# A new order table for a fused attention and GLU kernel, drawn up with later bank-free times

## The chip, the cores and the metric

One core of one Trainium2 chip runs the kernel. The metric is the device time of one execution in microseconds (us), as the median of repeated runs; a lower number is better. The profile is one further execution, traced by the hardware profiler.

## What is computed

Two branches read the same x (2048 tokens by 512 features, fp32) and are mixed by a gate:

```python
q = (x @ wq), 32 heads of 16;  k = x @ wk;  v = x @ wv      # one k and v for all heads
a = softmax(q k^T / 4) v, heads side by side, @ wo
b = (sigmoid(x @ w_gate) * (x @ w_up)) @ w_down              # 1792 hidden features
g = sigmoid((x * gate_w).sum(-1))
out = g * a + (1 - g) * b
```

## The kernel before

**Tiles and stages.** The tokens are cut into 4 blocks of 512. The 32 heads are cut into 8 groups of 4, which gives 32 units (block, group). For one unit the keys are cut into 16 chunks of 128. TensorE (PE) does five kinds of work, always into one of the eight PSUM banks of 128 x 512 fp32:

- `project` (L854): keys, values and queries from x, 12 full matmuls of 128 x 128 weights for each bank. It happens in the first 80 us only. The order calls it G.
- `maximum` (L1132): scores of one head, laid so that VectorE (DVE) can take the row maximum with one TENSOR_REDUCE (L1134). 2048 half matmuls, each on 64 rows of the array.
- `scores` (L1141): the scores again, transposed, with the maximum taken off inside the matmul. ScalarE (ACT) writes their exponentials p (L1143). Also 2048 half matmuls.
- `fill` (L1106): the GLU products and the output projection, 4404 half matmuls in chains of 12 to 36 that add up in one bank. ACT reads a finished bank of the gate product (L1115), DVE one of the up product (L1121), and ACT (L1082) or DVE (L1063) one of the products that go to the output.
- `pv` (L1005): p times the values, 4 matmuls of 32 columns for each chunk (the trace has two records for each). The order calls a chunk V. Chunks that follow each other without other work form a run and add up in one bank of their own. At the end of a run ACT copies that bank out (`finish`, L1012), and GpSimd (POOL) adds the copy to the unit's sum (`add_sums`, L1019). The copies of a unit after its first have two buffers (`vp`).

The three kinds of half matmuls use the upper or the lower 64 rows of the array, and two of them run side by side as a pair, one on each half. A chunk of `pv` uses all 128 rows and 32 columns at a time.

**What sets the order.** The string `ORDER` (L668) has one character for each step of PE. V and G are told above. A hexadecimal digit issues a pair: its quotient by 4 is the work of the upper half and its remainder that of the lower, with 1 for `maximum`, 2 for `scores`, 3 for `fill` and 0 for nothing. A point issues nothing. `plan` (L716) walks this string with the class `State`, which books a time in units of its own for each of PE, DVE, ACT, POOL and SyncE (SP). It decides from these bookings which bank is taken (`take`, L190: the one that comes free first, and it must be free by the booking), who empties a bank, and where the work of the other engines and the DMAs fall between the steps. The instructions of each engine then stand in this order, and semaphores guard every bank. So the bookings decide an order and nothing else; no time of the chip comes out of them.

**When a bank counts as free.** In `issue_m` (L512) and `issue_s` (L522) this stands as

```python
self.free[i] = self.on("dve", self.now + LATE, RED) + TAIL + FREE          # maximum, L516
at = self.on("act", self.now + LATE_A, EXP) + TAIL_A; self.free[i] = at + FREE_A   # scores, L528
```

`LATE` and `LATE_A` are the units from the issue of a matmul until DVE or ACT may begin, `RED` and `EXP` what the reader takes, `TAIL` and `TAIL_A` its end, and `FREE` and `FREE_A` a margin on top. `settle` and `gather` (L428, L458) use the same margins for the banks of `fill`, and `release` (L554) uses `FREE` for the bank of a run. The step of a run needs a bank that is free and four p of its chunk (`can_v`, L535).

Of the kernel before, what the change touches and what calls it, by code (L numbers as in the profile page):

```python
# [663 lines left out]


ORDER = (  # L668
    "GGGGGGG555G55G555G55......5G55GG555G55G555GG55G555GG5dddGff7f77ffffd757d.GG7fffdfffd7f7ffffdedee7edef7ef7b7b7b7b"
    "bdfedebdfbdb79ffef55VVVV7b76bfdbf9fbdef9fe7ededee7f6f7bdef6fdff7775VVV9deedef7edf9fbe77bfb7bb7bdff9edb7fedfd75dV"  # L670
    "VVVVGV6fede.edfef7efbb7f9fb7b7b7bfed9fbdb7fedbfed7d5VV655VVV7b7bb7fededbf9e7fbdededeef77b7ef9faf7d7f7ddVVVV5bb77"
    "bbbffde79fefededeede7bf77bfbd6fff7ddd5VVV566VV6ddefe7eedf6fbfe7b7b7b7bbdfbdfededbb7fedbf5VV555VVV97b7fbdbdbfb7eb"
    "fdedededeef76ffb76fef9f6fbf5V5a6V996VV696V559VVV7b7b7bbfdbdbedfe7edeeddee7fb7fed6feedf7777bVVVV9deeedf7fedb7bdef"
    "b7b7bb77eefddeedfef9b7ffdbddfedd5VVVVV6e9ff77bfb7b7bb77bfedbbdf6ff9f9ff.dd66VV659VV659VV7b7b7bbdfedbedfe79feedde"
    "e7f6f7bf9fbf6f6ffd5VVVVV7b97b7bbfdf9fee7efdedeede77efdbe7fee7feedfbdbfed9dVVVVV56fbfe7bfb7b7bb77bfbdafdbdf7bfedf"
    "de.56VV65aV6a5V955VVV97bbb77ffbdbdee7fededeede7f7b7bbfdbf9fbfb7e7aff775VVVV9dedfbdee7fedeeddef6fe7e7e7bfdbff775."
    "5VVVVV9deff9f6fbd6fedefb7b7b7bbdff9f9bf7ef97edefaV65eVVV959VV677bbfdfeeddee7f6ff797VVVdede7efb7b7b7bedbdff9eVVVd"
    "edede7ef6f6fbf97bfb7bb7bdff9f6efdbf6dbeff615.VVVVV6deededf7bf6feb7fbdb7bb7bbdfdfbdb7ef6edf5fdVVVVV5edeef7bfe7ede"
    "7e7bfb7b7bbdff9dbf6f9fedbf6fdV5a6V9aaVVVVV6dedef7ef6f6fbdbfb7e727b7bdef9fdbfbdef9f6f6f.9VV955VVV6edff6defb7ed6fb"
    "fe7b7bb7bdedfedfb7bf97edbfd4.9VV656VV5a5VV97bfdbdbe7f6fedefe7e763b7befdedefdbdefb7b79f.5VVV9a5V595VVV7b7afdedbf7"  # L680
    "b79fefbdedeedee77ff6f9fe7edb7bf7V95aV669V99aVV695VVV7b7afdf97efedef6fedb7b7bbdff96ffbd6fbffddd5VVVV677bbb7fdbfed"
    "bf6fededeede77fbfba7fdbf7fddd5VVVV767bbb7bffdedbe7fedededee7fb7f6ef7edbfd7f79VVVVV97bbb77fdef9f6fedefbde4ee7defe"
    "7dbf9fbb7f9ff55.VVVVVV7b79bffa7fdebdb7fededeedef7f6fe7e7bf9f9f6f7VVV969VV6edeedf7fb79fee7f9fb7b7bb7bfdedfbdef9f6"
    "ffd545.VVVVV96edffb7bf7edb7bbfdedeede7ef7defe7ebdb7bbf9VVVVV5baV9b7b7bb7fdfe7bedfedededee7ff6f67bfbdbfd7fd5VVVVV"
    "5edeeedfb7f6fe7bef7bb7b7bfddeefdbdbfa7f7eebV996V965VV5a9VV6a5VV6dedef7bfb79fbf9fb7edeede7ef7e7efdef97b7ffedefedd"
    "9VVVVV69f7bff6fb7b7bb7b7f9fedebdbf79ffefe5.6VV955VVV9b7b7fdbfb79fee7fededeede7ef7deef7ef67bffd9ffdedd5VVVVV67b7f"
    "bf9b7fe7b7bb7fededeedf7bbbd7ff5.5VVVVVdedede6ff6fb7bdb7efb7bb7bdef7edfedbf97bfed715.VV59aVVVV7b7bb5fee7fbdebdfbd"
    "eededef7b7fb7b79ff5efeedVVV659VV5bbb7fefdedede7efb7bf7b7b7VVV9fdeeddeedfe7b7be7V956VV977bbb7ffbd9fedbfedededee77"
    "fb7bfb7bf9fd7bfe7fbf67aVVVVV97defedefe7edeededfb7ef6f6fdbef7b79.dbVV955VVV7b7bb79b7ff9feedfededeede7fe76ffbdbf6b"
    "dff75V559VVVVV56efbfedf6fbd6fbfbde7b27bdfed7ebf7ededbfbfb.55VVVVV7b79b7fbfed6f9fedbfededee77ef7bdbfbfa7ffdd6Va95"  # L690
    "VV56aVVV5b7b7bfbdefb79fedefededee7f7bf6f9fb7bdefef.645VVV996V59aV569VVV7b7bb5fefbdb7bedfedededee77fbb7fb7bbddeed"
    "f5ca.VV666V59aV655VVVdede7ebdbf76fedbfe7b7b7bbdff9bdbfdb7eedeff585.VVVVV56b7.bfefdef9f6fedefb793bb7b7fbd6ff9eff9"
    "efdee5VV566VVVV5b7bb7fbdef9fb7eefdededeedbf7f6f6fafd7bff79VVVVV977b7bfeefd6fbf9f9fedeede7f7ef6fbd9fbf6ff75VVVVV9"
    "e9dff7ef6f9fef67efb7bb7bddfb9ffbde7ef9bffbfb67777VVVVV5bbfededefdededeed.7efb7edbfb7bdfbdf55VV655VVV67befdf9fb7b"
    "f6f9dbfeedede7ffe7b7bf9f6fbdef5VVVVV5b7bb7fef9f6fef9dbfedeede7fe77b7ef9fbf6ffddedeeedeVVVVV69fb7fb7fe7b7bb7b7f9f"
    "bdbdbef7f9efde.6eVV65aV9a5V596VVVV7b7bb7fededebde7f9fbd6ceedf7eef7bdbb7deb7fdb.5VV659VVV97b7bfdbf9fe7eb7defedede"
    "dbbf77bfe7e7edefbf2.65VV595VVVdedededeef7e7b7bb7fb7b.7bbdfbdb7edeed7feff7515VVV955VVV66fbfdf6fbdb7bdbfe7ededee7f"
    "f97eefdbf6dbbbf6VVVVV5eeffb7efbde7eedbf7b7b7b7eff9f9dbf9ffedf7d5VV569VVVV6b7bb7bfdfdbdbe7efdedeedef76ffe7bbf5bfa"
    "fd7dVVVVV7b7bbfdedededefb76ff75VVdede6ffb7b7b7bf9fefe5dVV79bb7b7bffdaf5fefededeede7fb7fbde76fbf9faf5c5.VVVVV6ded"
    "defbef76fef9fb7b7b7bbdf9ff6f9fbb7dedef5c9.VV666V5a9VVVV977bbbfdfbde7edbfe7eddeee7ff6f9faf7dbfe7bf6VVVVVV977bbfde"  # L700
    "bfdbdb7efbdedeede7bf77ebfdee77efbf15.5VVVVV59effb7bbf79fbf9fededdeee7fb7fb6f7eed7edbfbVV6a6VVVV5bbbfdb7def9faf7b"
    "fdedeeddf6fefe6f76fbef7bbbV969V5a5VVVVV6deeedf7dbf6fbb7fbde7b87bdfeddbfe76fefbdf7b.9aVV65aV95aVVVV6deeedf7ef7bd9"
    "fbfe7b7bb7bdedff97bfede7f7fd5VV556VVVdedeedfe7e7e7bdbfb7b7b7bbfddbefdbdbf6fedf75VV659VVV5aeff7edfedb7b7ef.edb7b7"
    "b7bfe7bfd9bdfbededf5c9VV666V65aV595VVVdedeb7bfde7e7efbfdb7b7bbdfedef6dbf6fef7f575VVVVdedee9dff6f6f9fbfb7b7b7bbdf"
    "edbdeef5fefe75VV97b57VVVVdededeedfe76fbbf7b7bb7b7bdf9ffedbbd7bdffdd5VV56aVV97b7fe7ef9fb79fefe7edeede7ffb6dfef9f6"
    "fbfb75VV555VVVVdede9fe7fb7e7edbbfdb7bb7bdff9b7efd6fef6ffdededddeeVVVVV67bf7e7efb7b7bb77bfbdafdedfedf9ff775.aVV96"
    "aVVVV5edeef7bdefbdee7fb7b7b7bbdbfddbfbd6fedeff75V655VVVVdeded6efe7fb79fefb7b7bb7bdfdef9fb7ef9dbfef616.VVVVV6dede"
    "dfb7ef6fe7bef7b7bb7bdbdfbddbfaf7deffd4a5.VV655VVVV5eededefbf7e7bdbdbfb7bb7bdfedee7dfef67bfbfa15.VV655VVVV59effb7"
    "bdbfede7bfb7edeede7f6fbdfe7eed7ffedbdafedbdVVVVV6f6b7fb7fbdb7b7bb7fbdbbddedefb7ebfde.aV6a6VV996V56aVVVV9ededffb7"
    "b7b7bdeedf6fbVVVdededbfb7b7bb7fbfedee6V56aVVV5b7bbb7fdbfafddbfededeede77effe7bdee7bb7fd5.35VVVVVdededeedef7e7bb7"  # L710
    "fb7b7bb7bdfdbe7dbfbdbf6eefe.2aVVaaaVVVaaaVVVbfbffbefefeebaVVeeeefffffbbbbaVVaaaVVaaaVVeefefbfffebaVVbbbbbfffafff"
    "eeeVaaaVVaaaVVeeffffbb8VVV"
)


# [532 lines left out]
```

## Time and profile before

| | |
|---|---|
| median of 3 runs | 1585.42 us (1584.21 to 1585.45) |
| the profiled execution | 1584.35 us, its span 1582.4 us |
| busy, share of the span | PE 99%, DVE 85%, ACT 77%, POOL 50% |
| instructions | 12910 matmul records, 2280 on DVE, 2415 on ACT, 713 on POOL |
| granted TensorE clock | 1.00 of full speed |

The 1.95 us between the span and the execution's own time lie around the program. A busy PE in this profile is a PE with some matmul under way, so waits inside a stream of matmuls must be read from the start times in the timeline and from the weight loads (PEld), whose idle time before them is recorded with its releaser.

### The profile page before, as it was taken

To read this page: it belongs to the slowest core of one execution; us is meant where nothing else is said; L and a number is where in the kernel's file an instruction comes from. 1 tells how busy PE (TensorE), PEld (TensorE's weight loads), DVE (VectorE), ACT (ScalarE), POOL (GpSimd) and SP (SyncE) were. 2 spreads that over 40 slices of the span, in tenths; PEclk is the share of its full clock that TensorE was granted. 3 is DMA by queue.
4 is the path that set the end of the run, shared out by engine and by line. 5 is a ranking of instruction groups with operands and counts; after the bars stand their busy time and mean duration, and the time that the engine had idled before them with its cause. 6 is when DMAs were issued, how large, how long until landed. Compare 5 with 4: busy or idle time off the path is not lost.

```text
span 1582.4 us, 33531 instructions
## 1 busy us (share of the span) xinstructions
PE 1572.6 (99%) x12910; PEld 1026.3 (65%) x12910; DVE 1337.5 (85%) x2280; ACT 1223.7 (77%) x2415; POOL 786.0 (50%) x713
## 2 busy tenths in 40 slices
...
DMA packets 62839, 102.94 MB, mean 65 GB/s; under 512 B 24412, under 2 KB 24668, under 8 KB 62680
## 3 DMA queue, kind: packets, MB, share of 16 engines
...
q14 instruction: 58, 0.48, 0.1%
...
## 4 chain that ended last, share of the span: by engine, by line
PE 97%; DVE 1%; ACT 0%; DMA 0%; SPq 0%; issue 0%; POOL 0%; DVEq 0%; ACTq 0%
PE bank L1106 33%; PE bank L1005 29%; PE bank L1132 17%; PE bank L1141 15%; PE bank L854 2%; DVE mx L1134 1%; SPq L967 0%; DMA qs<-qd 0%; DVE q L947 0%; ACT x L781 0%; PE bank L1187 0%; DVE x L787 0%; DMA wkv_raw<-wkv 0%; POOL wkv_s L757 0%; DVE wkv_stack L885 0%
## 5 line engine op out<-in xcount | busy, mean ns | idle before, releaser
L1134 DVE TENSOR_REDUCE mx<-bank 128x1 f32<-128x512 f32 x2048 | 1251.1, 681 | 173.1 <-PE bank L1132 109.5
L1143 ACT ACTIVATE p<-bank 128x512 f32<-128x512 f32 x2048 | 1036.7, 653 | 4.6 <-PE bank L1141 1.1
L1141 PE MATMUL bank<-qs,ks 64*128 64x512 f32 x2048 | 721.5, 400 | 0.0
L1132 PE MATMUL bank<-ks,qs 62*128 62x512 f32 x2048 | 682.5, 408 | 0.2 <-DMA qs<-qd 0.2
L1005 PE MATMUL bank<-p,v_aug 128*32 128x512 f32 x4096 | 477.5, 597 | 0.0
L1132 PEld LDWEIGHTS bank<-ks,qs 62*128 62x128 f32 x2048 | 338.3, 184 | 131.8 <-issue 50.9
L1141 PEld LDWEIGHTS bank<-qs,ks 64*128 64x128 f32 x2048 | 360.7, 185 | 83.4 <-ACT p L1143 18.4
L1012 ACT COPY ou<-bank 128x512 f32<-128x512 f32 x194 | 116.8, 602 | 281.9 <-PE bank L1005 195.6
L1019 POOL TENSOR_TENSOR ou<-ou,ou 128x512 f32<-128x512 f32 x163 | 210.0, 1288 | 210.8 <-ACT ou L1012 209.1
L1005 PEld LDWEIGHTS bank<-p,v_aug 128*32 128x32 f32 x4096 | 114.5, 109 | 254.6 <-issue 208.7
L1106 PE MATMUL bank<-wd,hl 64*128 64x512 f32 x1344 | 279.4, 392 | 0.1
L1106 PE MATMUL bank<-x,wu 64*128 64x512 f32 x1344 | 278.7, 391 | 0.0
L1106 PE MATMUL bank<-x,wg 64*128 64x512 f32 x1344 | 275.6, 392 | 0.0
L1106 PEld LDWEIGHTS bank<-wd,hl 64*128 64x128 f32 x1344 | 205.2, 185 | 19.7 <-issue 4.2
L1106 PEld LDWEIGHTS bank<-x,wg 64*128 64x128 f32 x1344 | 203.2, 185 | 16.8 <-issue 2.0
L1106 PEld LDWEIGHTS bank<-x,wu 64*128 64x128 f32 x1344 | 204.8, 185 | 14.3 <-issue 1.7
L1085 POOL TENSOR_TENSOR ba<-ba,pa_d 128x512 f32<-128x512 f32 x31 | 39.6, 1285 | 103.2 <-ACT pa_d L1082 103.2
L830 POOL CAST wg<-rg 128x1024 fp32r<-128x1024 f32 x27 | 28.1, 1039 | 124.8 <-PE bank L1106 69.1
L757 POOL TENSOR_TENSOR wd<-rd,wd 128x512 fp32r<-128x512 f32 x56 | 72.4, 1292 | 4.5
L757 POOL TENSOR_TENSOR hl<-h,hl 128x512 fp32r<-128x512 f32 x56 | 72.0, 1286 | 4.5
L1106 PE MATMUL bank<-wa,o 64*128 64x512 f32 x360 | 71.5, 393 | 0.0
L830 POOL CAST wu<-ru 128x1024 fp32r<-128x1024 f32 x27 | 28.1, 1040 | 82.4 <-PE bank L1106 76.1
...
## 6 DMA issues: line engine op xcount, KB each, us to landing
...
```

The lines of the kernel that those rows point to most:

```text
L757: lo.tensor_tensor(hl[:, 1, :], raw, f32(hl[:, 0, :]), op=ALU.subtract)
L830: nc.gpsimd.tensor_copy(WS[item][:, 0, :], raw)
L854: nc.tensor.matmul(ps, w[:, p, part(kc)], X[b, kc][:, q, :], start=i == 0, stop=i == 3 * KC - 1)
L1005: nc.tensor.matmul(ps[32 * j:32 * j + 32, :], v_aug[:, c, :], PT.pop((u, c, j)), start=start, stop=stop)
L1012: nc.scalar.copy(to, ps)
L1019: nc.gpsimd.tensor_tensor(SUMS[u], SUMS[u], PARTS_OF[u].pop(0), op=ALU.add)
L1085: nc.gpsimd.tensor_tensor(BA[b, t], BA[b, t], PA[b, t].pop(0), op=ALU.add)
L1106: ins = nc.tensor.matmul(banks[i], l, r, start=start, stop=stop)
L1132: nc.tensor.matmul(banks[i], qs_t[u % 3][r, pr, part(qt)], ks[r, kb * 512:(kb + 1) * 512], start=True, stop=True)
L1134: nc.vector.tensor_reduce(MX[u][:, pr, h, qt, kb:kb + 1], banks[i], axis=AX.X, op=ALU.max)
L1141: nc.tensor.matmul(banks[i], ks[r, part(c)], qs_t[u % 3][r, pr, :], start=True, stop=True)
L1143: nc.scalar.activation(p, banks[i], AF.Exp, scale=0.25)
```

## The change

Five of the planner's numbers are raised (`LATE` by 2 units, `LATE_A` by 4, `FREE` by 35, `FREE_A` by 5, `RED` by 2), and the string `ORDER` is another one, for which each `take` holds under the new numbers. The reference, the tiles, the functions that issue instructions and the number of matmuls stay. The diff, cut:

```diff
-LATE, LATE_A, FREE, FREE_A = 188, 196, 30, 55
+LATE, LATE_A, FREE, FREE_A = 190, 200, 65, 60
...
-RED, GATED, SUM, ENDS, INVERSE, LOWER = 258, 258, 285, 115, 70, 285
+RED, GATED, SUM, ENDS, INVERSE, LOWER = 260, 258, 285, 115, 70, 285
...
 ORDER = (
-    "GGGGGGG555G55G555G55......5G55GG555G55G555GG55G555GG5dddGff7f77ffffd757d.GG7fffdfffd7f7ffffdedee7edef7ef7b7b7b7b"
...
+    "GGGGGGG555G55G555G55........5G55GG555GGG555G55G555GG55Gff5fdfffff7ff75d..ddffffffff75fd7GG755Gb7bfedbbd7bfe7bdfe"
...
```

In the characters of the string: 512 V and 24 G stand in both. The runs of V are 182 before and 197 now; stretches of V or G, each with digits on both sides, are 193 and 209. Steps with one half alone (a digit with 0 on one side) are 26 and 4, points 43 and 15. The rows of each engine are as many on PE and SP, four fewer on DVE, 19 more on ACT and 19 more on POOL. All line numbers behind the string are lower by one in the changed kernel.

**Place one: PE, unit 20 (block 2, group 4), `pv` of chunks 8 to 12.** In a row of `pv`, p_9_0_1 is the tile of chunk 9 and head pair 0, 1. Before, one run holds chunks 8 to 12; the stretch from chunk 9 to chunk 10 reads

```order
L1005 MATMUL bank_79<-p_9_0_0_13631,v_aug 32x512
L1005 MATMUL bank_79<-p_9_0_1_13619,v_aug 32x512
L1005 MATMUL bank_79<-p_9_1_0_13624,v_aug 32x512
L1005 MATMUL bank_79<-p_9_1_1_13594,v_aug 32x512
L1005 MATMUL bank_79<-p_10_0_0_13647,v_aug 32x512
L1005 MATMUL bank_79<-p_10_0_1_13665,v_aug 32x512
L1005 MATMUL bank_79<-p_10_1_0_13640,v_aug 32x512
L1005 MATMUL bank_79<-p_10_1_1_13654,v_aug 32x512
```

and now

```order
L1004 MATMUL bank_76<-p_9_1_0_13621,v_aug 32x512
L1004 MATMUL bank_76<-p_9_1_1_13673,v_aug 32x512
L1131 MATMUL bank_79<-ks,qs_108 128x512
L1131 MATMUL bank_77<-ks,qs_108 128x512
L1131 MATMUL bank_72<-ks,qs_108 128x512
L1140 MATMUL bank_73<-qs_109,ks 128x512
L1140 MATMUL bank_74<-qs_109,ks 128x512
L1131 MATMUL bank_75<-ks,qs_108 128x512
L1004 MATMUL bank_78<-p_10_0_0_13685,v_aug 32x512
L1004 MATMUL bank_78<-p_10_0_1_13709,v_aug 32x512
L1004 MATMUL bank_78<-p_10_1_0_13641,v_aug 32x512
L1004 MATMUL bank_78<-p_10_1_1_13702,v_aug 32x512
```

The run ends behind chunk 9, three pairs of half matmuls follow, and chunk 10 begins a new run in another bank. Each end of a run brings one more copy on ACT (L1012 before, L1011 now) and one more addition on POOL.

**Place two: PE, the same unit, the run that holds chunks 2 to 4 before and 1 to 5 now.** Before, the last rows ahead of the run and its first row are

```order
L1106 MATMUL bank_77<-x_1_9220,wg_5_12653 128x512
L1106 MATMUL bank_78<-x_1_9220,wg_5_12653 128x512
L1106 MATMUL bank_77<-x_1_9220,wg_5_12653 128x512
L1132 MATMUL bank_76<-ks,qs_108 128x512
L1106 MATMUL bank_77<-x_1_9220,wg_5_12653 128x512
L1132 MATMUL bank_73<-ks,qs_108 128x512
L1132 MATMUL bank_72<-ks,qs_108 128x512
L1132 MATMUL bank_75<-ks,qs_108 128x512
L1132 MATMUL bank_74<-ks,qs_108 128x512
L1132 MATMUL bank_79<-ks,qs_108 128x512
L1005 MATMUL bank_78<-p_2_0_0_13292,v_aug 32x512
```

and now

```order
L1105 MATMUL bank_72<-x_1_9247,wg_5_12715 128x512
L1140 MATMUL bank_76<-qs_109,ks 128x512
L1131 MATMUL bank_74<-ks,qs_107 128x512
L1105 MATMUL bank_78<-x_1_9247,wg_5_12715 128x512
L1105 MATMUL bank_72<-x_1_9247,wg_5_12715 128x512
L1105 MATMUL bank_78<-x_1_9247,wg_5_12715 128x512
L1131 MATMUL bank_77<-ks,qs_108 128x512
L1105 MATMUL bank_78<-x_1_9247,wg_5_12715 128x512
L1140 MATMUL bank_73<-qs_109,ks 128x512
L1131 MATMUL bank_79<-ks,qs_107 128x512
L1004 MATMUL bank_75<-p_1_0_0_13328,v_aug 32x512
```

Before, the run takes bank_78, whose last writers are the gate products (L1106) a few rows above it, so that ACT must have read the gate out of it (L1115). Now the run begins one chunk earlier and takes bank_75, which no row shown above it writes; the gate's banks here are bank_72 and bank_78.

## Rows read from the trace of the kernel before

**Rows 1.** The page of before: span and busy time of each engine.

```profile
span 1582.4 us, 33531 instructions
...
PE 1572.6 (99%) x12910; PEld 1026.3 (65%) x12910; DVE 1337.5 (85%) x2280; ACT 1223.7 (77%) x2415; POOL 786.0 (50%) x713
```

**Rows 2.** The page of before: shares of the chain that ended last, by engine.

```profile
PE 97%; DVE 1%; ACT 0%; DMA 0%; SPq 0%; issue 0%; POOL 0%; DVEq 0%; ACTq 0%
```

**Rows 3.** Windows: us, busy of PE, PEld, DVE, ACT, POOL (x instructions), then clock.

```profile
600.00:1000.00 400.00, 399.95 (x3361) 262.82 (x3360) 348.05 (x591) 318.70 (x633) 199.50 (x180) 1.00 0.19 61
```

**Rows 4.** Timeline, PE, 705 to 711.7 us: start, us, instruction, merged count.

```profile
705.02 1.92 PE L1005 MATMUL bank<-p,v_aug 128*32 128x512 f32 x16
706.88 0.50 PE L1132 MATMUL bank<-ks,qs 62*128 62x512 f32 x2
707.21 0.40 PE L1141 MATMUL bank<-qs,ks 64*128 64x512 f32 x1
...
707.45 0.40 PE L1141 MATMUL bank<-qs,ks 64*128 64x512 f32 x2
707.78 3.64 PE L1005 MATMUL bank<-p,v_aug 128*32 128x512 f32 x32
711.35 0.50 PE L1132 MATMUL bank<-ks,qs 62*128 62x512 f32 x1
...
711.69 0.39 PE L1141 MATMUL bank<-qs,ks 64*128 64x512 f32 x1
```

**Rows 5.** Waits of PEld, ACT: us in total, times, longest.

```profile
PEld bank L1005 <- ACT p L1143: 22.6, 72, 0.9
PEld bank L1132 <- ACT p L1143: 22.1, 46, 0.8
PEld bank L1132 <- DVE mx L1134: 22.1, 38, 0.8
PEld bank L1141 <- ACT p L1143: 18.4, 36, 0.8
...
ACT ou L1012 <- POOL ou L1019: 15.2, 13, 2.4
...
PEld bank L1141 <- DVE mx L1134: 11.7, 35, 0.8
PEld bank L1005 <- DVE mx L1134: 10.6, 31, 0.4
```

**Rows 6.** Timeline, PEld, 1423.6 to 1425.5 us, around a run of two chunks.

```profile
1423.63 0.16 PEld L1005 LDWEIGHTS bank<-p,v_aug 128*32 128x32 f32 x8 [0.24 <-ACT gs L1115]
...
1425.48 0.18 PEld L1132 LDWEIGHTS bank<-ks,qs 62*128 62x128 f32 x1 [0.84 <-DVE mx L1134]
```

**Rows 7.** Timeline, 1050.4 to 1051.4 us, a run that waits for its bank.

```profile
1050.46 0.94 PE L1132 MATMUL bank<-ks,qs 62*128 62x512 f32 x5
1050.55 1.15 ACT L1115 ACTIVATE gs<-bank 128x512 f32<-128x512 f32 x2
...
1051.33 0.16 PEld L1005 LDWEIGHTS bank<-p,v_aug 128*32 128x32 f32 x8 [0.36 <-ACT gs L1115]
```

**Rows 8.** Timeline, 947.5 to 948.2 us, a pair that waits for its bank.

```profile
947.57 0.39 PE L1106 MATMUL bank<-x,wg 64*128 64x512 f32 x1
...
947.85 0.18 PEld L1132 LDWEIGHTS bank<-ks,qs 62*128 62x128 f32 x1 [0.21 <-DVE mx L1134]
...
948.19 0.39 PE L1141 MATMUL bank<-qs,ks 64*128 64x512 f32 x1
```

**Rows 9.** Timeline, PEld, the first and the last wait of that kind.

```profile
114.97 0.18 PEld L1141 LDWEIGHTS bank<-qs,ks 64*128 64x128 f32 x1 [0.16 <-DVE mx L1134]
...
1244.28 0.18 PEld L1132 LDWEIGHTS bank<-ks,qs 62*128 62x128 f32 x1 [0.19 <-DVE mx L1134]
```

**Rows 10.** Groups by line and form: busy, mean ns | idle before, releasers.

```profile
L1012 ACT COPY ou<-bank 128x512 f32<-128x512 f32 x194 | 116.8, 602 | 281.9 <-PE bank L1005 195.6 <-issue 32.7 <-POOL ou L1019 15.2
L1019 POOL TENSOR_TENSOR ou<-ou,ou 128x512 f32<-128x512 f32 x163 | 210.0, 1288 | 210.8 <-ACT ou L1012 209.1
```

More of the change, by code (lines that the diff above doesn't have):

```diff
@@ L668 @@
 ORDER = (
-    "GGGGGGG555G55G555G55......5G55GG555G55G555GG55G555GG5dddGff7f77ffffd757d.GG7fffdfffd7f7ffffdedee7edef7ef7b7b7b7b"
[L670 to L712, printed above, removed]
+    "GGGGGGG555G55G555G55........5G55GG555GGG555G55G555GG55Gff5fdfffff7ff75d..ddffffffff75fd7GG755Gb7bfedbbd7bfe7bdfe"
@@ new lines @@
+    "dedeedfe76fee7fedbfbb777.5VVVV9dedef7bf9f6fee7f9fb7bb7bdfbdfbd6fef7ffdd55VVV656VV6ddefb7efbde7eedfb7b7bb7bdf9fbd"
+    "f6feeedffb79VV555VVV97bfe7edf9fe7bb7fbdededee7f6ffe7edbf7ff7755VVVV6fdedef9f9fedeb7fb7bb77bbfd9ffbdb7ef9fddf5dVV"
+    "VVV67fb7bbdfb7ef6bdefdedeedef7e7fb7bf6f9fffd55VVVV7b7b7b7bfed9fbdedefedeede7f7b7efe7bedf5f5f7VVVVVdededb7efe7eed"
+    "7bfb7b7b7bbfd9fbdf6fef97fdfd5VV695VV566VVdedeedef7b7e7bf9f9f7bbb7bffde7edbfed6fbff55VVVV6a5V9edef7def6f6fedb7bfb"
+    "7b7bbdf9ffbdbde7ef6fed7V599VV566VVV9edef7f9fe7ef6edb7fb7bb7bfdbdbdfede7bfe7f5dVV695VV596VVdedb7bfe7bbd7bf9ffeded"
@@ new lines @@
+    "ee77bfb7bdee7fed6ff57VVVVVdedededefb7ee77bbf7b7b7bbfd9fbfd9fb7effede5VV655VVV977b7bfef9f9fb7efededeede7f6ff6fbdb"
+    "edff7b79V5a9VV566VVV5ededefbfb79fef6f6f7bbb7bfddef9fb7bdbfdddf6VVVVV7b7bb5fbfed6fbf9fededeedef7b77bfe7eedfb76fdV"
+    "659VVVV696Vdede5eeffe7bb7defb7b7bb7bdfdbfedeb7dbfedb7dVVV655VVV97b7fbfededeed7bf6fafbVVVdedeef7b7b7bb7fededf57VV"
+    "dede6edff6fb7edbbf7b7b7bbdff9fbdedefa7fdf57VVVVV7b7b7bbdf9fbde7efededeede7f6ffb7edefdf7bb57VV955VVV96dffe7efbd6f"
+    "eb7fedb7b7bbfdbdeef7dbfb7edfe5V9a6VVVV56aV6ddefbdefb76fede7bf7bbb7bfddebdfef9e7effb75VV596VVVVdedee6dffb7ef6f9fb"
@@ new lines @@
+    "7b7b7bbfdf9dbfbdeee7fff95Va5aVV695VVV5b7b7bfefbdeb7ed7efedeede7fed7efb7bf9fefbb9V569VV656VV599VV97b7fe7bfbdaf7f9"
+    "efdededee7f6f7bfe7bdefe7f97V965VV96aVV996VVV9ef7f97bfbbd7bfedfededee7e7f6fbf6dbfbdb7f5dVV655VVV5b7bfedbf9f6fbf6f"
+    "9fededee7fe7dbfb7edfff7795VVVV977bbff9fedaf7f97efedeedef76ffe7bdbf97bffd5VVVV7b79fedbfe7edb7bfbdededee7fb7bf7b7b"
+    "deffde5dVVVVV7b7e7ef9f9fb7bed7efededee7fb7fbdb7b7efdd5feVVVV65aVV5edefbe7f6f9fe7bfedb7b7bbdf9ffb7bdefbdfded6V696"
+    "VV6a9VV6a5VVVdedeedef76f6fbf6fb7b7bb7bdfedfedbedbdfb76f7VVVV9deedff6fede7be7fb7b7b7bbfdbdfed9fbdefff755VVV956VVV"
@@ new lines @@
+    "7b7bb5fbfbd9fedef6fedeeddefb7fb7e7ee7dbfbf5VV965VVV5eef7edefe79fbf6fbdbb7bb7fdfbdbdb7efedffd55VVVV767bfbdbfedbf6"
+    "f6fbdedeede7f7efb79fbbde7fef9VV656VVVV5edefedefb7ee7f9fb7b7b7bbdfdedbfe7bf97ffdd6VV695VVVV97b7fedbfb79fbedf6fede"
+    "dee7f6ffe7edefbfb7b79VV595VVb779bffbdebdfe76ffededee7fb79feb7dbfede7f75VV9a6VVVVdededee7f6fbf6dbfb7b7b7bbfd9fbdf"
+    "bde7bfede7dVVV656VV596VVdedef6fb7b7b7bdbfedef9VVV7b7bfbdededeedfb7bff65VV976ffbdefb7bf9f9e7fededeef7e7edfb7bb7fb"
+    "d9feV955VVVV5b7bfb7bfedb7eedfe7edededef6f7bfe7bfa7ffd75VV95aVVVVde9def7bfb7b7bf9fe7edeedef7e7efde7bfb97ff75VV955"
@@ new lines @@
+    "VVV7bdef6f9fbde7edefe7b7b7bbdfedfed6fb7bbffee9V965VVVVV6ddeedeff6fb7ef6bf7b7bb7bdfbdfededefb9f7f79V966VVVV59aV7b"
+    "7b7bfbd9fafde7fedeeddee7f7bfedee7b7f9f6f7VV959VV5a6VVVdadbf7edfe7af7defe7b7b7bb7fbdefdededbef7f5bV999V654aVV5aaV"
+    "V659VV7b7b7bbfd9fede7bfedededeef7f6fe7edeff7b7779VVVV5ededefbfedbbde7fb7b7bb7bfdf9bfdb7ef5ffddd5VVV656VV5edeeef7"
+    "fbdef6bdb7fb7bb7bdf9ffbdb7eedb7fdedVVVVV767bfee7f9fedbb7fe7eddeedfbf6fb7bf9dedff77aV565VVVVVdede6ffb79fe7edbf6fb"
+    "b77bbdff9f9f9fe7bfefee9V659VVVV977bb7fbfedebdb7fededeede7fe7ef7b7eddfd77b7VVVVV97fbf9f6f9fb7bdbfededeedef7b7b7fb"
@@ new lines @@
+    "db7efefed5VV655VVVde6edf7efbdbf6f97efb7bb7bfddefb7edbf97effd6V969VVVVV7b7bdbfed6fbf6bdfbdeeddee7fb7fb79fbf6fefee"
+    "5VV5a9VVVV7b5bfb7bfedb7edbfedededeef7e7ef7bdef7fd7775VVV599VVdede6f7efbde7ebdfb7b7b7bbfd9fedf6fbedeffb7aV955VVVV"
+    "797bfe7ef9f9fb7efbdedededef6fef7b7b7efe7f79VVVVV9dfb7ebdfb7bdb7befdeddeee7fb7f6f6fef9fbfbd9VV665VV569VVVdedaf7f6"
+    "fedaf7bdfe7b7bb7bdfedfb7bdbf6ffded9V666VVVVVdedededefb76feb7fb7b7b7bbdf9ffbdb7efbdede7dVVV655VVeddeef7b7b7b7bfbd"
+    "eefe5VVVdedeef7b7bb7b7f9ffded5VV97bb7b7ff9feedf97efedeede7fb77bfede7edf7d77VVVV6ddedefefb79fedbfb7b7bb7bfdbdb7fe"
@@ new lines @@
+    "def9fe7f5eVVV695VVde5eedfefe76fbf6bf7b7bb7bfddbefd9fbdefe7f79V659VV56aVVVV9edef7f6f9fef6defb7b7bb7bfdbdbfdbdef6f"
+    "bdef5VV656VVVVdededef6f6feb7f9fb7b7b7bb7fbdfed9fbdbdeffe5V996VVVV7b677bfbfbdedeb7fededeeddbf7bfb7e7ef6fedbebV69a"
+    "VV966VVVVV5edeeefdfb7edb7efb7b7b7bbfd9ffedbdb7efbdf5eV6a6VV59aVV695VV96ffbdb7fbdb7bf6fedeedeedbf77fbf6fbdede7f75"
+    ".VV955VVV7b7bb77bfbdedfdefededede7efe7bde7bfe7ff7759VV959VV5b7bbb7ff9fedeb7fededeedef76ffe7edbfbdb7f57VV955VVV69"
+    "9V9b7fe7defb7bf9f6f9feedede7f6ff6f9fee7fb76f7VVVV999VVdedeeddee7fbf97bbf7b7bb7bf7fe6dfeedf9fefbb5VV569VVV6edef7d"
```

7 lines of the change are left out of this document (added).

## The prediction

> **What bounds the kernel now.** I read the page first, then the chain, the windows, the waits, and last the timeline around single events. The page shows PE busy for 1572.6 of 1582.4 us, far ahead of DVE (1337.5) and ACT (1223.7) [rows 1], and 97% of the chain that ended last is PE's own [rows 2]. In the middle of the kernel PE is busy for 399.95 of 400 us at a granted clock of 1.00, which is the 2.4 GHz level [rows 3]. So the time is the length of PE's own stream. Three things make it up: the matmuls themselves, the changes between pairs (two halves of the array) and chunks of `pv` (column strips), and the weight loads that stand before a bank which DVE or ACT has not emptied yet. The change leaves the first alone, adds to the second and can take from the third. How the other engines share their time matters only where PE waits for them.
>
> **The matmuls.** Their number is the same: 8500 half matmuls, 512 chunks, 24 steps of projection. What falls is the number of steps with one half alone, from 26 to 4. If every lone half cost a whole step, 22 of them would be 11 pairs less, at 0.24 us each from start to start (707.21 to 707.45) [rows 4], or 2.6 us. At the other end is nothing, since each half of the array has its own stream and the partner of a lone half can begin the next step early. I take 0.2 us off, near that end, because the count of half matmuls is what fills PE. The points (43 to 15) issue nothing and cost nothing by themselves.
>
> **The changes between pairs and chunks.** There are 193 stretches of chunks or projections between pairs before and 209 now, 16 more. A run of two chunks takes 1.86 us to the next pair (705.02 to 706.88) and one of four 3.57 us (707.78 to 711.35), so a chunk is 0.855 us [rows 4]. From the start of the last pair ahead of the run of four to the second pair behind it are 4.24 us (707.45 to 711.69); two pairs at 0.24 and four chunks at 0.855 would be 3.90. A run therefore costs **0.34 us** for its two changes [rows 4], and 16 more cost 16 x 0.34 = **+5.4 us**, wholly on the path. The Trainium skill speaks against the change here: by "TensorEngine Tiling (Array Packing)", section "Key Properties", a change of tiling mode drains TensorE, while a change of tile alone does not. The rows above bear it out as far as it goes; by it alone the change is a loss of those 5.4 us, while the rows below show waits at the start of runs that can be won back.
>
> **What the runs bring to the other engines.** Each of the 16 runs adds a copy on ACT (0.602 us) and an addition on POOL (1.288 us) [rows 10]: 9.6 us on ACT and 20.6 us on POOL. The planner also gives three parts of the output sum to ACT and POOL that DVE had. ACT has 359 us without work, POOL 796 [rows 1], and neither is PE's bound, so I cost this at nothing. What hides it is that slack; if it were gone, a copy would hold up the exponentials queued behind it on ACT. No DMA is added: SP has the same number of rows, and the transfers are the same.
>
> **The waits at the start of a run.** A run needs a bank, and the copies, the gate's activations and the exponentials that empty it are ACT's. Weight loads of `pv` waited 72 times for ACT's p and 31 times for DVE's maxima, 33.2 us in all [rows 5]. Not all of it is waiting: 0.24 us stand before a run that hardly waits [rows 6], and 103 x 0.24 = 24.7, so at most 8.5 us are lost there. One that waits shows 0.36 us, behind the gate's two activations (1050.55, 1.15 us) [rows 7], so a wait costs about 0.12. That is the run of place two; the new order gives it a bank that the gate doesn't hold. The tables can be counted for this: a run's first step takes a bank that ACT empties, within 20 units of the booking, 34 times before and 5 times now. 29 x 0.12 = 3.5 us is what these could bring. I take three quarters of it, **-2.6 us**, as some of the 34 start on time and some of the longer bookings don't. The ends are 0 and -8.5.
>
> **The waits of pairs.** Weight loads of `maximum` and `scores` waited 155 times for p or for the maxima, 74.3 us together [rows 5]. 58 of these are merely the first load behind a run, with 0.84 us during which the chunks ran [rows 6]: 48.7 us. 97 are left, with 25.6 us. What such a wait costs PE is seen at 947.57: two steps take 0.62 us (to 948.19) in place of 0.48, so about 0.14, though the load stood idle for 0.21 [rows 8]. Of the 46 that wait for DVE, nine hold PE up so, the first at 114.97 and the last at 1244.28 us [rows 9]; most are hidden by the matmuls under way. Since no bank of DVE is taken within the 35 added units any more, I count all nine as gone: 9 x 0.14 = **-1.3 us**. ACT's 51 are different. Their margin grows by 5 units (9 with `LATE_A`), and takes within 20 units of the booking are no fewer (130 before, 145 now); I take **-0.5 us** for them, near zero. The ends for both are 0 and 97 x 0.14 = -13.6.
>
> **The sum.** -0.2 + 5.4 - 2.6 - 1.3 - 0.5 = **+0.8 us**, against the profiled execution of 1584.35 us: 1585.15. The median of the runs shown is 1.07 us above that execution, so the forecast is **1586.2 us**, 0.05% over the median. A measurement of this kernel can tell about 0.2%, 3.2 us, from no change: below 1582.2 is faster, above 1588.6 slower.
>
> **Rivals.**
> *The runs cost and nothing comes back (slower).* Place: the two changes of each added run. Price: 5.4 us, less 0.2 for the lone halves. It decides when the waits saved stay under 2.0 us. For it: the price is a fixed one and every run pays it, while most waits for banks are hidden [rows 8]; it is also how the time goes if the margins are only numbers in the planner and banks come no sooner on the chip. Against it: 34 starts with a tight bank become 5. Time: 1585.4 + 5.2 = 1590.6. The Trainium skill's rule on the drain, taken alone, gives this case: "TensorE: Matmul & The Clock Gate", section "Single matmul latency", puts a drain at about 175 ns; an estimate from that page is 2 x 0.175 x 16 = 5.6 us for the runs, beside 5.4 by the rows. Chance 0.14.
>
> *Most waits go (faster).* If all starts are free of waits (-8.5) and a quarter of the pairs' upper end goes (-3.4), the sum is 5.2 - 11.9 = -6.7: 1578.7. It decides when over 8.4 us are saved, nearly twice what the counted cases hold. For it: the two upper ends add up to 22 us, and a wait can come from a stall before it. Against it: so few of the 97 reach PE. Chance 0.19 for all of it that ends below 1582.2.
>
> *ACT waits for POOL (slower).* A unit's copies have two buffers. ACT already stood idle 13 times for POOL's addition, 15.2 us, 1.17 each [rows 5, 10]. Runs of one unit that begin within four steps of the end of the last are 77 before and 93 now. If each of the 16 more made ACT wait 1.17 us and PE with it, that is 18.7 us: 1604.9. A bank or a p would have to be missing at once for PE to feel it. Chance 0.03.
>
> **Chances and range.** The forecast's own case, within 3.2 us of the median, has 0.64: the known price and the counted savings nearly cancel, and to leave the band the savings would have to come to under 2.0 or over 8.4 us in place of 4.4. Faster 0.19, slower 0.17 (0.14 and 0.03). The range runs from 1581.0, which takes part of the faster case, to 1590.6, where nothing comes back; about 2 in 10 lie outside. The forecast's own range is 1583 to 1589.
>
> **What would show it.** Right, if the copies on ACT are 210 in place of 194 and a run still costs about 0.34 us; if the loads of `pv` wait less often for ACT though there are more runs; and if waits of the pairs' loads for DVE, other than the 0.84 behind a run, go from 46 to under 20. Wrong, if waits of pairs for DVE stay near 46, if the starts of runs lose as much as before, or if PE shows gaps behind a DMA or a POOL result that it did not wait for before. A clock below 1.00 in the middle would void the comparison.

## The result and the profile after

| | before | after |
|---|---|---|
| median of 20 runs each, same chip | 1584.38 us (1583.53 to 1586.49) | 1586.87 us (1585.12 to 1588.45) |
| ratio, 95% interval | | 1.0014 (1.0008 to 1.0020) |
| the profiled execution, its span | 1584.35, 1582.4 us | 1588.15, 1586.2 us |

The change costs 2.5 us, or 1.3 to 3.2 by the interval: inside the 0.2% that the forecast counts as no change, and inside its range. The forecast had +0.8. The sum of the working came near; two of its parts did not, and they nearly cancel, which is in part luck.

The page of after: span, busy time of each engine, and the shares of the chain that ended last.

```profile
span 1586.2 us, 33588 instructions
PE 1574.0 (99%) x12910; PEld 1015.9 (64%) x12910; DVE 1340.2 (84%) x2277; ACT 1237.1 (78%) x2434; POOL 809.7 (51%) x732
PE 96%; DVE 2%; POOL 1%; DMA 1%; ACT 0%; SPq 0%; issue 0%; DVEq 0%; POOLq 0%; ACTq 0%
```

Against [rows 1, 2] PE's share of the chain falls from 97% to 96% and POOL and a DMA have 1% each. That one per cent is where the surprise lies. The mean granted clock is 0.998 in place of 1.000; where it fell stands below, under the late wait.

**Runs, as priced.** The timeline of after, PE, around a run of four chunks (start, us, instruction, merged count):

```profile
705.83 0.40 PE L1131 MATMUL bank<-ks,qs 62*128 62x512 f32 x1
706.16 3.64 PE L1004 MATMUL bank<-p,v_aug 128*32 128x512 f32 x32
...
710.06 0.39 PE L1105 MATMUL bank<-x,wu 64*128 64x512 f32 x1
```

From the last pair ahead of the run (705.83) to the second behind it (710.06) are 4.23 us, as the 4.24 before [rows 4]. A run costs what it did, and there are 16 more.

**Copies and additions, as counted.** The groups of after by line and form (busy us, mean ns of one | idle before, releasers):

```profile
L1018 POOL TENSOR_TENSOR ou<-ou,ou 128x512 f32<-128x512 f32 x179 | 230.5, 1288 | 171.8 <-ACT ou L1011 169.2
L1011 ACT COPY ou<-bank 128x512 f32<-128x512 f32 x210 | 127.5, 607 | 271.9 <-PE bank L1004 110.0 <-issue 90.8 <-POOL hl L755 22.6
```

210 copies in place of 194 [rows 10], each as long as before.

**Waits.** The view of waits, PE's weight loads and one row of ACT (total us, times, longest):

```profile
PEld bank L1140 <- ACT p L1142: 29.8, 70, 1.7
PEld bank L1131 <- ACT p L1142: 27.6, 55, 0.8
...
PEld bank L1131 <- DVE mx L1133: 11.1, 18, 0.8
PEld bank L1004 <- ACT p L1142: 10.2, 29, 0.6
...
PEld bank L1140 <- DVE mx L1133: 5.2, 7, 0.8
...
PEld bank L1105 <- POOL o L755: 2.3, 1, 2.3
PEld bank L1105 <- SPq L1109: 1.9, 3, 1.0
...
PEld bank L1105 <- POOL o L756: 1.1, 1, 1.1
...
ACT ou L1011 <- POOL ou L1018: 15.0, 12, 2.5
```

To be read against [rows 5]. Loads of `pv` wait for p 29 times in place of 72. Pairs wait for DVE's maxima 25 times in place of 73; 18 of the 25 are the first load behind a run, whose 0.84 us are no wait [rows 6], so 46 real ones became 7. Pairs wait for ACT's p more often: 125 rows in place of 82, or 81 in place of 51 without the 0.84. ACT waits for POOL as before (15.0 us, 12 times; it was 15.2, 13). The two rows of L1105 that wait for POOL's o had no counterpart before. The one that waits for SyncE (SPq) had: 3 times too, 1.2 us in all, the longest 0.5. The longest wait for ACT's p, 1.7 us, is not ACT's doing; it is read below, with the clock.

**The balance.** I added PE's steps from start to start through both timelines:

| | us |
|---|---|
| 16 more runs, less the lone halves | +5.2 |
| starts of runs: 374 ns from the last pair to `pv` before (181 cases), 353 after (197); over the 325 of a run that waits for nothing, 8.9 us before, 5.5 after | -3.4 |
| pairs: mean step 233.7 ns before, 232.7 after | -3.9 |
| late starts: 2.0, 0.8 and 0.9 us between 1561 and 1566 us, 0.8 at 963 us | +4.5 |
| start-up: first matmuls slower in this execution | +1.5 |
| sum, beside the spans' own +3.8 | +3.9 |

Only the sum of the second and third rows is firm. Counted to the start of the later half of the last pair, the starts of runs gain 1.6 us, and the pairs the rest. The pairs' row also hides some 0.9 us of slower steps behind the late starts, so the waits saved come to 7.3 us by the table and to about 8 without those.

The last row but one isn't the change's. PE's timeline from 4 to 12 us, first after, then before:

```profile
7.79 3.45 PE L853 MATMUL bank<-x,wkv_s 128*128 128x512 f32 x9
11.09 1.08 PE L853 MATMUL bank<-x,wq 128*128 128x512 f32 x4
```

```profile
7.33 2.33 PE L854 MATMUL bank<-x,wkv_s 128*128 128x512 f32 x9
9.49 2.69 PE L854 MATMUL bank<-x,wq 128*128 128x512 f32 x11
```

This piece of the program is the same in both kernels. The same nine matmuls take 3.45 us in one execution and 2.33 in the other. The trace's record of the granted clock begins at 10.24 us in the first and at 4.80 in the second, both at 1.00; before that no row shows it, so that the lower clock made them slow is argued only. For it speaks that in all thirteen traces a late record (10.2 to 10.7 us) goes with a late start of the second group (11.1 to 11.4) and an early one (4.3 to 6.4) with an early start (9.3 to 9.6). The start of that group fell near 9.4 or 11.2 us in both orders (9.32 and 11.27 in two of the experiments on the new order). Of the 1.6 us here 1.5 are left at 37 us. Without them the spans differ by 2.3 us, close to the 2.5 of the medians.

**The late wait.** PE's weight loads of after near the end, then the chain of after in the same stretch (start, us, what):

```profile
1561.06 0.18 PEld L1105 LDWEIGHTS bank<-we,o 64*128 64x128 f32 x1 [2.30 <-POOL o L755]
...
1562.41 0.18 PEld L1105 LDWEIGHTS bank<-we,o 64*128 64x128 f32 x1 [1.06 <-POOL o L756]
```

```profile
1554.11 0.02 SPq L1109
...
1554.83 4.16 DMA bc<-rd
...
1559.07 1.28 POOL vd L1053
...
1560.40 0.62 POOL o L755
...
1561.09 1.29 POOL o L756
```

These fills of the output projection (`we`, o) need the last division of the attention, on POOL (L1053, then the two parts of o). That needs the inverses spread over the rows by a DMA (bc, L1048). SyncE issues that DMA, and ahead of it in SyncE's queue stands an empty instruction that waits for PE: `CROSS` (L1109), which hands a sum from the one half of the array to the other. SyncE's own timeline of after shows the hold-up, 6.8 us behind the DMA before it:

```profile
1547.47 0.40 SPq L1042 DMA_DIRECT2D rd<-rc  x1
1554.25 1.10 SPq L1048 DMA_DIRECT2D bc<-rd  x2
```

Before, SyncE was held up much the same, for 5.5 us (SyncE's timeline of before):

```profile
1548.92 0.45 SPq L1043 DMA_DIRECT2D rd<-rc  x1
1554.43 1.08 SPq L1049 DMA_DIRECT2D bc<-rd  x2
```

The division ended at 1561.66 + 1.29 = 1562.95 us (POOL's timeline of before):

```profile
1561.66 1.29 POOL L757 TENSOR_TENSOR o<-vd,o 128x512 fp32r<-128x512 f32 x1
```

But PE came to those fills only at 1567.13, and did not wait for o (PE's weight loads of before; the 0.84 is that of a first load behind a run):

```profile
1567.13 0.18 PEld L1106 LDWEIGHTS bank<-we,o 64*128 64x128 f32 x1 [0.84 <-issue]
```

So the hold-up is old; what is new is that the order reaches the fills earlier: 25.1 us ahead of the end (22.6 in experiment 8, where nothing holds PE up behind them) in place of 15.3. PE's timeline of after, ahead of and between these loads:

```profile
1558.81 0.39 PE L1105 MATMUL bank<-wa,o 64*128 64x512 f32 x2
...
1561.40 0.39 PE L1105 MATMUL bank<-we,o 64*128 64x512 f32 x1
```

From start to start, less the 0.23 us of a step, PE comes 2.0 us late to the first of these fills and 0.8 to the third, and the step behind each is 0.1 longer: 3.0 us. The other late start is one load that waits for `CROSS` itself, 0.8 us lost:

```profile
962.96 0.18 PEld L1105 LDWEIGHTS bank<-x,wu 64*128 64x128 f32 x1 [0.98 <-SPq L1109]
```

**The clock behind the wait.** The wait brings a second loss. A window of after: us, busy of PE, PEld, DVE, ACT, POOL, then the granted clock (0.50), DMA share, GB/s:

```profile
1563.30:1566.70 3.40, 3.40 (x18) 1.03 (x14) 1.06 (x2) 2.26 (x5) 0.00 (x0) 0.50 0.02 5
```

The granted clock fell from 1.00 to 0.50, from 2.4 to 1.2 GHz, at 1563.31 us, just behind the two late starts, and rose again at 1566.72. The runs of `pv` around it, first after, then experiment 8, in which no fill waits and the clock stays at 1.00:

```profile
1554.98 1.93 PE L1004 MATMUL bank<-p,v_aug 128*32 128x512 f32 x16
...
1563.69 1.93 PE L1004 MATMUL bank<-p,v_aug 128*32 128x512 f32 x8
...
1566.97 1.93 PE L1004 MATMUL bank<-p,v_aug 128*32 128x512 f32 x16
```

```profile
1556.05 1.92 PE L1004 MATMUL bank<-p,v_aug 128*32 128x512 f32 x16
...
1561.54 1.06 PE L1004 MATMUL bank<-p,v_aug 128*32 128x512 f32 x8
...
1563.48 1.92 PE L1004 MATMUL bank<-p,v_aug 128*32 128x512 f32 x16
```

The run of one chunk takes 1.93 us in place of 1.06. The first pair behind it starts 0.9 us late for that reason; its load shows 1.66 us idle, twice the usual 0.84, and that is the 1.7 us put down to ACT's p above. From the first of these three runs to the last are 11.99 us in after and 7.43 in experiment 8. Of the 4.6 us by which these differ 3.0 are the wait; the other 1.5 or so are the lower clock's. In 15 of the 20 executions of the changed kernel the mean granted clock is 0.997 or 0.998 (median of these 1587.0 us) and in five 0.999 or 1.0 (1586.0); in the 70 of the kernel before that ran beside the experiments it is never under 0.999.

### The profile page after: what moved, and what is told of

It reads as the page before. It is cut to its first block, busy times and chain, and to the rows that moved or that the text cites. A ratio compares the mean times of both kernels' runs of the same rounds, so it can differ in the third digit from the quotient of the medians.

```text
span 1586.2 us, 33588 instructions
## 1 busy us (share of the span) xinstructions
PE 1574.0 (99%) x12910; PEld 1015.9 (64%) x12910; DVE 1340.2 (84%) x2277; ACT 1237.1 (78%) x2434; POOL 809.7 (51%) x732
## 4 chain that ended last, share of the span: by engine, by line
PE 96%; DVE 2%; POOL 1%; DMA 1%; ACT 0%; SPq 0%; issue 0%; DVEq 0%; POOLq 0%; ACTq 0%
PE bank L1105 32%; PE bank L1004 29%; PE bank L1131 17%; PE bank L1140 15%; PE bank L853 2%; DVE mx L1133 1%; DMA bc<-rd 0%; SPq L966 0%; DVE q L946 0%; POOL wd L756 0%; POOL wg L830 0%; DMA qs<-qd 0%; ACT x L780 0%; PE bank L1186 0%; DMA wkv_raw<-wkv 0%
## 5 line engine op out<-in xcount | busy, mean ns | idle before, releaser
L1140 PE MATMUL bank<-qs,ks 64*128 64x512 f32 x2048 | 729.8, 400 | 0.0
L1011 ACT COPY ou<-bank 128x512 f32<-128x512 f32 x210 | 127.5, 607 | 271.9 <-PE bank L1004 110.0
L1018 POOL TENSOR_TENSOR ou<-ou,ou 128x512 f32<-128x512 f32 x179 | 230.5, 1288 | 171.8 <-ACT ou L1011 169.2
L1105 PE MATMUL bank<-x,wu 64*128 64x512 f32 x1344 | 276.2, 392 | 0.6 <-SPq L1109 0.6
L1105 PE MATMUL bank<-wd,hl 64*128 64x512 f32 x1344 | 274.5, 392 | 0.1
L1105 PE MATMUL bank<-x,wg 64*128 64x512 f32 x1344 | 268.8, 392 | 0.0
L1105 PEld LDWEIGHTS bank<-x,wu 64*128 64x128 f32 x1344 | 202.4, 185 | 25.5 <-issue 5.9
L1105 PEld LDWEIGHTS bank<-wd,hl 64*128 64x128 f32 x1344 | 202.9, 185 | 20.6 <-issue 4.2
L1105 PEld LDWEIGHTS bank<-x,wg 64*128 64x128 f32 x1344 | 199.0, 185 | 21.8 <-POOL hl L755 2.5
L978 POOL CAST ms<-mm 128x16 fp32r<-128x16 f32 x32 | 6.3, 196 | 139.5 <-DVE mm L971 139.5
```

Of the source, the lines that this page charges most:

```text
L1011: nc.scalar.copy(to, ps)
L1018: nc.gpsimd.tensor_tensor(SUMS[u], SUMS[u], PARTS_OF[u].pop(0), op=ALU.add)
L1105: ins = nc.tensor.matmul(banks[i], l, r, start=start, stop=stop)
L1140: nc.tensor.matmul(banks[i], ks[r, part(c)], qs_t[u % 3][r, pr, :], start=True, stop=True)
```

## Experiments

Kernels that were run side by side share the runs of before: median 1584.21 us for the first four, 1584.73 for the next four, 1584.61 for the last three. Nothing of the computation is left out in any.

**1, 2. The empty instruction off SyncE, in both kernels.** For the fill that stands in front of the last DMA, DVE issues it:

```diff
-            CROSS[j.key, x] = nc.sync.nop()
+            CROSS[j.key, x] = (nc.vector if (j.kind, j.b) == ("a", NB - 1) else nc.sync).nop()
```

> The changed kernel, with SyncE's empty instruction between the two halves of the last output projection (block 3) given to DVE, so that the last broadcast of the inverse sums no longer stands behind it on SyncE. Theory (a new wait): the changed order reaches the last fills sooner than their tile, and PE stands still for some 3.7 us near 1560 us for it, because that broadcast was issued late; with the edit the wait goes, 1586.9 - 3.7 = 1583.2 us (1582.3 to 1584.2), and the trace shows no PE step over 0.5 us late after 1540 us. Rival (the runs alone cost the difference, and the late wait belongs to the one traced execution or returns elsewhere): 1586.9 us (1586.0 to 1587.8).

Measured on the changed kernel: 1583.47 us (1581.72 to 1584.70), ratio to before 0.9993 (0.9984 to 1.0002); 3.4 us less than after. Its chain near the end:

```profile
1545.10 4.46 DMA rd<-rc
...
1549.57 0.53 SPq L1048
...
1550.15 4.50 DMA bc<-rd
```

> The kernel before with the same edit on SyncE's empty instruction. Theory (a new wait): its order comes to the last fills after their tile is there, so the edit gives nothing, 1584.4 us (1583.6 to 1585.2). Rival (SyncE held up by that instruction costs every order): 1580.5 to 1582.

Measured on the kernel before: 1584.34 us, ratio 1.0000 (0.9991 to 1.0009). In the changed kernel the DMA now leaves 4.5 us behind the one before it (1545.10 to 1549.57), as soon as that has landed, and not 6.8. Its loads of `we` still stand idle for 0.43 and 1.06 us, but the clock stays up: in none of the 11 executions is its mean under 0.999. The two runs of its trace between which after takes 11.99 us:

```profile
1552.56 1.93 PE L1004 MATMUL bank<-p,v_aug 128*32 128x512 f32 x16
...
1561.14 1.92 PE L1004 MATMUL bank<-p,v_aug 128*32 128x512 f32 x16
```

These are 8.58 us, 3.4 less than in after, as much as the medians differ by. Before, where PE comes late, the same edit is worth nothing. The late wait is the order's, and once it is shortened the two kernels can't be told apart.

**3, 7. More runs, nothing else.** In the order before, 16 (then 23) runs are cut in two by moving three of the pairs behind them into the run:

```diff
-VVVVV6e9
+VV6e9VVV
```

> The kernel before with 16 of its runs cut in two by moving the three pairs that follow a run into it, all else kept. Theory (a run has a fixed price): 16 more runs cost 16 x 0.34 = 5.4 us, 1584.4 + 5.4 = 1589.8 us (1588.8 to 1590.8), with 210 copies on ACT. Rival (a run's price is mostly a wait that more frequent runs spread or hide): 1584.4 to 1587 us.

> The kernel before with 23 of its runs cut in two (16 gave +6.4 us by the runs, with an interval of 3.5 to 7.4). Theory (a fixed price for a run, 0.34 us by the rows): 1584.2 + 23 x 0.34 = 1592.0 us (1591.0 to 1593.2). Rival (the price is 0.40 us or more, as the medians of 16 cuts say): 1593.4 us or more.

Measured: 16 cuts 1590.61 us, ratio 1.0035 (1.0022 to 1.0047), +6.4 us or 0.40 per run; 23 cuts 1590.67 us, 1.0034 (1.0021 to 1.0046), +5.9 us or 0.26 per run. The 23 missed their number by being too cheap. The price of 0.34 from the rows lies between the two medians. The interval of the first, 0.21 to 0.47 per run, holds it; that of the second, 0.14 to 0.32, ends just under it. The traces agree better with each other. From the first run of `pv` to PE's last row (L1187) are 1483.56 us before, 1487.84 with 16 cuts and 1489.96 with 23: 0.27 and 0.28 per cut. The traced execution of the 16 cuts had merely begun 1.5 us later (first run at 92.64 us in place of 91.12), as after had. So more runs cost some 4 to 6 us and give nothing by themselves; why a cut costs a little less than the 0.34 of the rows is not shown. The Trainium skill's rule that a change of tiling mode drains TensorE ("TensorEngine Tiling (Array Packing)", section "Key Properties") agrees with this in sign; the page gives no price.

**4. The new order with the old five numbers.**

```diff
-LATE, LATE_A, FREE, FREE_A = 190, 200, 65, 60
+LATE, LATE_A, FREE, FREE_A = 188, 196, 30, 55
```

(and `RED` back to 258.)

> The changed order string with the five numbers of before. Theory (the string alone makes the difference, the numbers only let the search find it): the same as the changed kernel, 1586.9 us (1586.0 to 1587.8). Rival (the numbers act by the choice of banks and of who adds a part): over 1 us away from the changed kernel.

Measured: 1586.42 us, ratio 1.0011 (1.0002 to 1.0020), as the changed kernel within the noise. For a given string the numbers do nothing that these runs can tell; the string makes the difference. The trace adds something on the clock. The same two runs of `pv` as above:

```profile
1553.30 1.92 PE L1004 MATMUL bank<-p,v_aug 128*32 128x512 f32 x16
...
1564.06 1.92 PE L1004 MATMUL bank<-p,v_aug 128*32 128x512 f32 x16
```

These are 10.76 us, 1.2 less than in after. The fills wait here too (the loads stand idle for 2.6 and 1.1 us), but the granted clock stays at 1.00. So the wait does not always bring the fall.

**5, 6. All of the margin used up.** `take` gives the free bank that came free last, not first, so that a bank is taken as soon as its booking lets it:

```diff
-        i = self.free.index(min(self.free))
-        assert self.free[i] <= self.now
+        i = self.free.index(max(at for at in self.free if at <= self.now))
```

> The kernel before with the same order string and numbers, but each take uses the free bank that came free last, not the one that has been free longest. The steps of PE stay; takes of a bank within 30 units (DVE) of the booking go from 184 to 341, within 20 units (ACT) from 130 to 240. Theory (banks taken close behind the margin of 30 cost PE a wait now and then, and that is what the wider margins save): slower by about 3 us, 1587.3 us (1586 to 1589), with more waits of pairs' weight loads for DVE's maxima. Rival (nearly all such waits are hidden by the matmuls under way, and the saving has another source): 1584.2 us (1583.4 to 1585.2).

> The changed kernel with the same edit of the take. Its banks of DVE have 35 units more in hand, so takes near the booking (136 to 376 within 30 units) should still find them empty; ACT's have 5 more. Theory (the margin of 65 covers DVE's waits): within 1 us of the changed kernel, 1587.2 us (1586.2 to 1588.2). Rival (the margin matters little, how many banks lie idle matters): slower by as much as the kernel before is slowed by the same edit, about 3 us, 1590 us.

Measured: on the order before 1590.12 us, ratio 1.0034 (1.0021 to 1.0046), +5.4; on the new order 1589.91 us, 1.0029 (1.0019 to 1.0038), +3.0 over after. Both missed their numbers, and the second came out at its rival's 1590 us. The waits of the two, the order before first:

```profile
PEld bank L1131 <- DVE mx L1133: 48.5, 103, 1.0
...
PEld bank L1140 <- DVE mx L1133: 26.5, 89, 1.0
```

```profile
PEld bank L1139 <- ACT p L1141: 34.4, 102, 1.7
...
PEld bank L1130 <- ACT p L1141: 20.4, 64, 0.9
```

With a margin of 30 it is DVE's banks that come late: 192 rows in place of the 73 of before [rows 5]. With 65 it is ACT's, whose margin grew by 5 only: 166 rows in place of 125. But the edit moves both kinds of bank, so a cleaner pair follows.

**9, 10. The margin of DVE's banks alone.** `take` gives the bank that DVE emptied last if one is free, and ACT's oldest otherwise (`of_act` marks the banks that ACT empties):

```diff
-        i = self.free.index(min(self.free))
-        assert self.free[i] <= self.now
+        i = min((i for i in range(8) if self.free[i] <= self.now),
+                key=lambda i: (1, self.free[i]) if self.of_act[i] else (0, -self.free[i]))
```

> The kernel before, where a take uses the bank that DVE emptied last as long as one of DVE's is free, and else the oldest of ACT's. Takes of a bank of DVE within 30 units of the booking rise from 184 to 342 as in the fifth experiment, those of ACT's stay word for word as they were (130 within 20 units). Theory (of the 5.4 us that the fifth experiment lost, nearly all is DVE's margin of 30, as its trace shows waits of pairs for DVE going from 56 to 154 and for ACT only from 51 to 56): 1584.6 + 4.5 to 5.5 = 1589.6 us (1588.4 to 1590.6). Rival (it was the choice among ACT's banks): 1584.6 us (1583.6 to 1586).

> The changed kernel with the same edit. DVE's banks are taken as close behind their booking as in the sixth experiment (377 within 30 units, 136 before the edit), ACT's as in the changed kernel. Theory (35 more units cover DVE's banks, and what the sixth experiment lost, 3.0 us, is ACT's margin, which grew by 5 units only: its waits of pairs for ACT went from 81 to 151): within 1 us of the changed kernel, 1586.9 us (1586.0 to 1587.9). Rival (idle banks matter, not margins): 1589.9 us, as in the sixth.

Measured: on the order before 1589.69 us, ratio 1.0030 (1.0020 to 1.0041), +5.1; on the new order 1588.47 us, 1.0020 (1.0011 to 1.0029), +1.6 over after, a little above what was expected. So a bank taken 30 units behind DVE's booking costs time, and one taken 65 units behind it costs little. Counted load by load, without those of 0.84 us, pairs wait for DVE 160 times in the first trace and 13 times in the second. The 1.6 us of the second are mostly not DVE's either. Its trace loses 2.4 us against after. Of these 1.2 are lost up to the run at 1554.85 us, 0.9 of them in one run near 864 us of which a load waits for ACT's p. The other 1.2 come behind 1554.85 us, where the granted clock is 0.50 from 1561.1 to 1567.9 us, twice as long as in after. The 35 units are real margin. In the order before they were seldom needed, since `take` gives the oldest bank.

**8, 11. The last division on DVE as well.** On top of the edit of 1 and 2:

```diff
-        nc.gpsimd.tensor_tensor(vd, vd, bc, op=ALU.mult)
+        on = nc.vector if u == NU - 2 else nc.gpsimd
+        on.tensor_tensor(vd, vd, bc, op=ALU.mult)
...
-        OT[b, g // 2] = split(vd, o, nc.gpsimd.tensor_copy, nc.gpsimd)
+        OT[b, g // 2] = split(vd, o, on.tensor_copy, on)
```

> The first experiment's kernel (SyncE's empty instruction of the last projection on DVE) with the last division of the attention sums on DVE in place of POOL (three operations that take 3.2 us on POOL). Theory (in the first experiment PE still waits for this division, 0.43 us before its first part and 1.06 us before its second, in the weight loads near 1557 us): faster by 0.8 us, 1583.5 - 0.8 = 1582.7 us (1581.9 to 1583.4), below the kernel before. Rival (DVE's own sums of the output stand in front of it, or the wait moves on to ACT's exponentials): 1583.5 us (1583 to 1584.5).

Measured on the new order: 1582.69 us (1581.90 to 1584.64), ratio 0.9986 (0.9977 to 0.9994). This is below both kernels: 2.0 us under before and 4.2 under after. Its timeline shows the division's first step on DVE and the fill behind it, which no longer waits:

```profile
1557.68 0.69 DVE L1054 TENSOR_TENSOR vd<-vd,bc 128x512 f32<-128x512 f32 x1 [10.03 <-DMA bc<-rd]
...
1560.08 0.39 PE L1106 MATMUL bank<-we,o 64*128 64x512 f32 x1
```

> The kernel before with both edits of the eighth experiment (SyncE's empty instruction of the last projection and the last division on DVE). Theory (the kernel before never waits there, so what the eighth experiment is faster by comes from the changed order's saved waits): 1584.6 us (1583.8 to 1585.4). Rival (the edits speed up any order's tail): 1582.7 us.

Measured on the order before: 1585.62 us, ratio 1.0006 (0.9998 to 1.0015). No gain, and a little above what was expected. Its timeline tells of a loss of its own: the division now stands on DVE ahead of a sum that empties a bank (L1064), and a pair waits for that:

```profile
1561.36 0.69 DVE L757 TENSOR_TENSOR o<-vd,o 128x512 fp32r<-128x512 f32 x1
1561.97 0.74 DVE L1064 SCALAR_TENSOR_TENSOR ba<-bank,gsig,ba 128x512 f32<-128x512 f32 x1
1562.77 0.29 PEld L1142 LDWEIGHTS bank<-qs,ks 64*128 64x128 f32 x3 [1.39 <-DVE ba L1064]
```

So the 2.0 us of the best version are not two edits that any order could have had: with the same edits the new order stands 1585.62 - 1582.69 = 2.9 us under the old. About 1 us of these 2.9 is that loss of the old order (0.9 us at the end of its trace); a DVE queue that puts the division elsewhere was not tried.

## Why the prediction was right, and where its working was wrong

- **What bounds the kernel** held: PE is busy 99%, the clock was at its upper level in the middle of the kernel (it fell only for 3.4 us near the end), and every gain and loss above is read from the start times of PE's own steps.
- **The matmuls, -0.2 us for lone halves**: too small to be read by itself; it stands in the balance as forecast, with the runs, and no run shows it alone.
- **The changes between pairs and chunks, +5.4 us**, held. The price of 0.34 us per run is the same in the rows of after, and cutting runs without any other edit gave 0.40 and 0.26 by the medians, 0.27 and 0.28 in the traces.
- **The waits at the start of a run, -2.6 us**: right in mechanism; the size isn't settled. The trace gives -3.4, or -1.6 if counted to the later half of the pair ahead. The waits of `pv` for ACT fell from 72 to 29 though there are more runs.
- **The waits of pairs, -1.3 and -0.5 us**: mis-sized. Pairs gained 3.9 us or more. The 46 waits for DVE went to 7, as "under 20" said, but I priced only the nine that a late start showed plainly. The smaller delays of the others were taken as hidden, and they weren't all. That ACT's waits rose from 51 to 81 didn't undo this. Experiments 9 and 10 show the mechanism (a tight margin behind DVE costs, a wide one little); that the 3.9 us are all its doing is argued from the counts.
- **What the runs bring to the other engines, costed at nothing**: this is the step that failed, in its sentence "No DMA is added: SP has the same number of rows, and the transfers are the same". It counted the queue's rows and did not ask when PE comes to what they deliver. The new order comes to the last fills about 7 us earlier, and the chain of SyncE, DMA and POOL ahead of them was as late as ever: 3.0 us of waiting, 1.5 more at the lower clock that came behind it, and 0.8 at 963 us where a load waits for SyncE. The clock was in the prediction only as a thing that would void the comparison, not as a price of a wait. Experiment 1 gives 3.4 us back, experiment 2 shows that before had nothing to give.
- **The sum**: waits brought about 7.3 us in place of 4.4, and 4.5 us of late starts were lost that I had not counted. Hence +0.8 forecast and +2.5 measured. That the two misses nearly cancel is luck.
- **Rivals.** That the runs cost and nothing comes back is refuted: the runs alone gave 1590.6 us, the change 1586.9. That most waits go (over 8.4 us saved) came near in its saving and not in its time; with the late wait mended and the division moved, the time went to 1582.69. ACT's waiting for POOL didn't grow (15.0 us). The text's own sign of error, gaps of PE behind a POOL result that it did not wait for before, is the one that came.

Open: why a cut costs 0.27 or 0.28 us in the traces and a run 0.34 by the rows, how the waits saved divide between starts of runs and pairs, and why the clock fell behind the wait in some executions and not in all.
